# Maxima of the experts' scores: broadcast to all partitions and subtracted in PSUM, instead of a product with a row of ones

## The chip, the cores and the metric

The kernel runs on one core of a Trainium2 chip. The metric is the device time in microseconds of one execution, as the median of several. A core has five engines that run their own queues of instructions: TensorE (PE in the profile; PEld is its weight load), VectorE (DVE), ScalarE (ACT), GpSimd (POOL) and SyncE (SP, which here issues all DMAs but one).

## The reference

Two stages follow each other. The first is attention in clusters for 4 x 8 heads of 768 positions and 64 channels. The second, which the change is about, takes the first one's output as `x` (4 x 768 x 512) and computes for each of four experts a causal attention with one head of 64 channels, weighted by a gate:

```python
for e in range(E):
    q = x @ wq[e]
    k = x @ wk[e]
    v = x @ wv[e]
    scores = scale * (q @ k.transpose(0, 2, 1))
    scores = np.where(causal, -1000000000.0, scores)
    scores = scores - scores.max(-1, keepdims=True)
    a = np.exp(scores)
    a /= a.sum(-1, keepdims=True) + 1e-09
    ye = a @ v @ wo[e]
    for kk in range(K):
        mask = topk[:, :, kk] == e
        out += mask[..., None] * w[:, :, kk:kk + 1] * ye
```

The weights `wq` and `wk` are scaled up some 53 times, so the scores are large and the maximum of each row has to be taken off before the exponential.

## The kernel before

The work is cut into 24 steps. Steps 0 to 15 are the first stage, each a pair of heads of one batch. Steps 16 to 23 are the experts: four batches times two pairs of experts, so a step holds two experts (`h` = 0, 1), one in partitions 0 to 63 and one in 64 to 127. 128 x 128 products in full width (projections, line 773; values, 813; output, 1305) use the whole array. The products of two experts of 64 channels use it in two halves of 64 rows, side by side.

In an expert step the scores are made twice. First with the query on the partitions (line 970, `moe_maxes`), so that DVE can reduce each row to its maximum: a custom instruction that adds the causal mask and takes the maximum on the diagonal block (line 978), a plain reduction elsewhere (981). The 12 columns of maxima (`M6`) are transposed by PE (1076), copied from PSUM with the sign turned (`mr`, 1082 or 1085), and one small DMA puts them as a row each into partitions 0 and 64 of a tile `qm`, whose other partitions are zero. Then the scores are made once more with the key on the partitions (line 1003, `moe_scores`), as the softmax's sum and the product with the values need them. Here four terms add up in PSUM: three for the product of numbers split in a high and a low part, (kh, qh), (kl, qh) and (kh, ql), and as the fourth a product of a tile `kone`, which holds ones in partitions 0 and 64 and zeros elsewhere, with `qm`. It adds minus the maximum of each query to each key. ACT then takes the exponential straight out of PSUM (1017), POOL cuts the diagonal block to the causal part (1158), PE multiplies with the values (1191), and DVE or POOL adds up the sums (375, 376).

A step has nine such score tiles (`hf` is the half of the queries, `kc` the block of 128 keys): five of 2 x 384 columns, two of 2 x 256 and two of 2 x 128. Each takes a pair of PSUM's eight banks (`bank2`, four pairs), out of the same eight that all other products use.

The order of all operations on all engines is written out by hand: `SEQ` lists some 3,700 numbers of operations, with a letter where an operation goes to another engine than its first choice (`a`, `d`, `p` for ACT, DVE, POOL), and `SLOT` says which bank or buffer each gets. `Plan.run` issues the operations in that order, and each engine works through its own in sequence. While the scores and sums of one expert step run, the projections of the next and the output of the one before stand between them.

Of the kernel before, what the change touches and what calls it, by code (L numbers as in the profile page):

```python
# [10 lines left out]
def _warn_once_fixed(msg, *args, **kwargs):  # L11
# [26 lines left out]
23 15 64 0 14 5 4 32 28 40 45 46d 47d 48p 41 43 27 6 37 38 42d 49 50 51 52 1 13 53 55 56 12 57 231 234 25 232 20 222  # L38
223 225 224 2 31 22 19 227 228 34 394 44p 70 39 58 59 60 61 399 400d 235d 30 62 63 233d 67 68 69 66 229 24 9 395 396
77 78 79 80 81p 82p 71 237 238 36 35 3 239 29 8 21 16 73 33 65 7 401 397 72 74 76p 75p 10 11 104 90 108 100 17 88 18  # L40
26 240 241 89 109 242 243 403 106 406 407 404 405 101 92 93 105 244 96 97 111 245 409 410 107 98 102 256 99 114 115
86 411 91 94 95 87 103 110 257 252 253 566 83 152 153 173 148 149 168 169 85 84 130 131 157 174 158 126 127 112 122
123 128 129 575 54 230p 246 248 249 418 247 113 163 124 138 125 139 254 164 258 260 132 133 422 421 166 167 255p
398p 161 162 259p 412 413 150 151 146 147 154 226p 251 402p 423 171 172 134 136 118 155 120 121 135 119 116 156 160
176 159 165 170 175 117 137 140 141 310 311 281 298 414 415 142 143 177 299 285 304 305 282 306 307 144 145 416 417
261 269 270 300 200 201 207 208 424 425 426 427p 263 428 429 197 419 301 420 202 203 264 286 236 267 268 180 198 191
430 432 433 431p 277 278 182 183 302 195 308 309 181 250 262 196 184 185 275 276 205 192 206 292 279 280 303 271 186
187 188 571 296 297 293 290 294 295 189 190 193d 199 204 209 576 577 578 579 283 284 265 266 572 273 288 194 210 211
573 272 289 291 312 274 287 313 460 435 436 314 315 462 463 480 482 483 567 568 434 474 481 443 457 458 441 442 569d
475 581 582 212 213 444 737 592 593 178 179 461 214 215 447 439 355 372 356 373 379 380 437 438 362 363 440 583 357  # L50
325 584 448 585 326 346 364 358 365 327 367 368 344 345 472 331 316 317 318 359 360 347 332 453 454 574p 570p 594
353 354 361 366 586 587 369 370 445 466 468 469 377 378 455 456 467 473 329 322 446 330 341 476 477 342 323 319 324
588 589 908 470 471 216 374 375 336 334 320 321 337 328 464 595 596 738 599 600 335 601 371d 602p 591 746 449 478
479 339 450 597 598p 742 743d 451 452 459 382 383 340 349 739 333d 338d 465 484 485 486 376d 381d 343d 348 590 603
604 217 649 650 635 408 647 648 605 487 740 741p 749 750 747 628 624 625 629 620 636 621 218 909 945 384 748 752 351
352 653 654 626 627 385d 386 744 763 745p 764 765 387 534 616 617 549 550 525 526 527 651 753d 614 615 531 633 634
528 532 608 609 350 544 545 631 632 536 641 642 652 529 530 612 610 611 503 504 613 516 517 541 542 754 755 497 518
519 535 491 537 546 547 492 493 494 495 496 756 539 488 637 638 489 511 513 490 514 540 533 220 643 954 618 498 499
580 219 538 644 619 512 757 500 758 645 646 501 502 506 606 607 507 388 759 760 639 622 551 552 761 950 951d 508 509
770 766 767 768 771 772 775 762 774 505 510d 515d 520d 946 554 521 773 769 947d 543d 640 623 655 630 656 657 555 952  # L60
1116 389 658 522d 955 956 957 958d 781 785 814 818 779 819 815 780 390 922 776 786 782 548 553 556 557 523 524 558
1125 948 972 971 923 392 391 953p 949p 973 960 961 820 804 799 800 805 707 708 705 812 824 821 825 698 808 674 675
# [3 lines left out]
718 1117 978 979 980 974 975 560 976d 982 1121 681d 981 827 828d 1122d 983 977 561 829 984 751 714d 719d 723 724d  # L66
725 726 685 683 692 693 686d 691d 1123d 1124p 1128 1129d 1118 1119 562 1126 1127 830 1022 1023 1028 1005 993 994
1006 694 727 728 1131 1132 695d 729 1296 1120p 1144 1142 564 563 730 1029 1024 989 990 855 856 999 1000 1030 1031
1025 839 840 841 848 833 834 835 849 1133 1134 853 1135 869 870 831 832 871 872 836 1016 843 844 888 889 1007 837
838 995 1017 996 845 846 854 858 1136 1137 1143 1001 1002 860 861 842 847 987 988 731 1008 850 851 1026 1138 1139  # L70
1140 1010 997 998 1011 1141 565 1287 959 859 863 864d 852 857 862 1145 1149 1150 1151 1152p 985 891 892 1003 867 868
1146 1147 1148p 1154 732 1153 1027 1014 1004 881 1015 1155 991 883 884 1018 1019 893 894 1020 1032 878 879 992 986
1009 1033 1021 873 1012 1013 1034 886 1044 874 875d 1292 882 876 877 880d 885d 1297 1288 1035 1299 1300 1293 1036
1037 887 1289 896 1290 1298 1302 890d 1458 895d 898 899d 1294 1295p 1303 865 1467 866 900 1314 733 1313 1291p 897
# [4 lines left out]
1319 1326 1060d 734 1195 1066 1189 1067 1071 1065 1070 1181 1470 1076 903 904 1130 736 1190 1072 1471 1196 1185 1186  # L79
1086 1203 1182 1162 1204 1163 1087 1081 1082 1468 1469 1178 1197 1179 1180 1083 1088d 1093d 1463 1096 1097 1187 1188  # L80
# [3 lines left out]
1362 1363 1333 1334 1475 1227 1228 1255 905 1466p 1462p 393 1486 1250 1251 1476 1356 1357 1340 1477 1234 1235 1248  # L84
1249 1229 1230 1257 1256 1258 1254 1259 1270 1271 1360 1372 1373 1337 1358 1239 1260 1240 1261 1265 1266 1264 1478
1479 1215 1216 1217 1352 1224 1225 1212 1480 1481 1361 1634 1359 1109 1638 1482 910 1483 1301 1345 1338 1346 1370
1371 1272 1273 1630 1213 1214 1221 1491 1492 1493 1222 1341 1353 1376 1487 1488 1267 1489 1490 1237 1223 1226d 1494
1495 1496 1635d 1631d 1268 1269d 1238 1242 1275 1276 1110 1342 1523 1351 1377 1378 1111 1497 907 1243 1274 1231d
1236d 1241 1379 1112 1113 1114 1636d 1632 1655 1639 1514 1640 1524 1525 1516 1517 1641 1386 1545 1546 1541 1542 1535
1536 1642 1644 1645 1277 1278d 1244 1800 1245d 1279 1643 1656 1280 1637p 1633 1657 1533 1534 1502 1503 1526 1393  # L90
# [3 lines left out]
1540 1658 1659 1281 1428 1429 1521 1662 1663 1664d 1665 1430d 1435d 1654 1809 1282 1660 1666 1667 1283 1403 1518  # L94
1498 1441 1442 1404 1436 1437 1504 1543 1544 1397d 1440d 1519 1445d 1413 1547 1661 1402d 1668 1446 1499 1505 1414
# [111 lines left out]
    vt="010101011010101011011100010110",  # L207
    mx="0110100110101010101001010110010101010101",
    ssb="010101010101010101010101",
    acc="010101010101010101010110011010011001",  # L210
    avu="010101010101010101011010",
    r="0101010101010101010110010",
    xt="0100010101010101010101100110100110100",
# [3 lines left out]
    g="01320123",  # L217
# [1171 lines left out]
```

## Time and profile before

| | before |
|---|---|
| median of 3 runs | 673.76 us (673.62 to 674.83) |
| the profiled execution | 673.12 us, its span 671.4 us |
| PE busy | 663.9 us (99%) |
| PEld busy | 513.6 us (76%) |
| DVE busy | 543.4 us (81%) |
| ACT busy | 340.1 us (51%) |
| POOL busy | 302.7 us (45%) |
| granted TensorE clock | 0.999 of 2.4 GHz |

A busy share is the time in which an engine had an instruction in work. Matmuls are pipelined: the next starts before the last ends, so what a product costs in a stream is the distance of two starts and not its own duration. The distance between the end of the span and the execution's own time is 1.7 us.

### The profile page before, as it was taken

The numbers are of one execution on the slowest core, as the hardware profiler recorded it, in microseconds if no ns is written. First come the engines' busy times: TensorE is split into PE (matmuls) and PEld (weight loads), VectorE is DVE, ScalarE is ACT, GpSimd is POOL, SyncE is SP. The second block draws the span as 40 slices with busy tenths as digits, with TensorE's granted clock in tenths as the row PEclk, the third lists the DMA queues.
The fourth block names the chain that finished last, engine by engine and source line by source line (L and its number), as shares of the span: only waits on it lengthen the run. The fifth ranks groups of instructions, "written<-read, shape, count | busy, mean of one in ns | idle before, by whom it ended". The sixth has DMA issues, their size and how long they took to land.

```text
span 671.4 us, 13404 instructions
## 1 busy us (share of the span) xinstructions
PE 663.9 (99%) x4817; PEld 513.6 (76%) x4817; DVE 543.4 (81%) x1210; ACT 340.1 (51%) x791; POOL 302.7 (45%) x275
## 2 busy tenths in 40 slices
PE   9999999999999999999999999999999999999997
PEld 6778677677677677687687688969969969968975
DVE  7998998988799979999999988669576857786543
ACT  4556466467576466465575543264324334426423
POOL 4885555473664563536577132236132365304200
PEclk9999999999999999999999999999999999999999
DMA  6796868687678578577767533220322010221232
GB/s 200 182 219 140 207 167 181 169 206 195 161 205 202 143 199 230 149 176 193 164 173 189 142 97 99 69 72 2 96 95 73 28 50 25 74 73 50 95 121 95
DMA packets 70735, 90.79 MB, mean 135 GB/s; under 512 B 21088, under 2 KB 60428, under 8 KB 70668
## 3 DMA queue, kind: packets, MB, share of 16 engines
q1 hardware_dynamic: 70524, 89.90, 51.4%
q8 instruction: 38, 0.62, 0.4%
q14 instruction: 29, 0.24, 0.1%
q10 hardware_dynamic: 144, 0.03, 0.0%
HBM read 36.54 MB, written 12.91 MB: 74 GB/s over the span
## 4 chain that ended last, share of the span: by engine, by line
PE 87%; DVE 10%; issue 1%; ACT 1%; POOL 1%; DVEq 0%; ACTq 0%
PE banks L1191 19%; PE banks L773 10%; PE banks L1055 10%; PE banks L1134 8%; PE banks L1135 8%; PE banks L1003 6%; PE banks L813 5%; PE banks L1305 5%; DVE acc L376 3%; PE banks L516 3%; PE banks L1215 2%; PE banks L970 2%; DVE mx L1061 2%; PE banks L1138 1%; PE banks L1143 1%; PE banks L547 1%
## 5 line engine op out<-in xcount | busy, mean ns | idle before, releaser
L1061 DVE TENSOR_REDUCE mx<-banks 128x1 f32<-128x384 f32 x384 | 190.7, 547 | 13.2 <-PE banks L1055 11.8
L1134 PE MATMUL banks<-tq,tk 128*128 128x384 f32 x324 | 113.9, 352 | 0.0
L1055 PE MATMUL banks<-tk,tq 80*128 80x384 f32 x384 | 111.3, 358 | 0.1
L1135 PE MATMUL banks<-tq,tk 97*128 97x384 f32 x324 | 109.7, 339 | 0.0
L1153 ACT ACTIVATE p<-banks 128x384 f32<-128x384 f32 x144 | 65.4, 497 | 25.9 <-PE banks L1135 21.1
L1055 PEld LDWEIGHTS banks<-tk,tq 80*128 80x128 f32 x384 | 67.5, 189 | 11.6 <-DVE mx L1061 5.2
L1134 PEld LDWEIGHTS banks<-tq,tk 128*128 128x128 f32 x324 | 61.2, 189 | 6.4 <-issue 1.5
L1135 PEld LDWEIGHTS banks<-tq,tk 97*128 97x128 f32 x324 | 61.6, 190 | 0.0
L370 ACT ACTIVATE avu<-banks 128x384 f32<-128x384 f32 x34 | 16.5, 487 | 72.1 <-PE banks L1191 67.3
L978 DVE CUSTOM_DVE_ANT_0 banks<-banks,tri 128x384 f32<-128x384 f32 (+4 forms) x96 | 45.6, 530 | 5.7 <-PE banks L970 4.8
L1191 PE MATMUL banks<-p,vt 128*64 128x384 f32 x288 | 50.0, 490 | 0.0
L1266 POOL TENSOR_TENSOR xt<-avu,rb 128x384 f32<-128x384 f32 x28 | 28.2, 1023 | 48.2 <-DMA rb<-rd 27.4
L1153 ACT ACTIVATE xl<-banks 128x384 f32<-128x384 f32 x88 | 42.1, 500 | 8.6 <-PE banks L1135 7.7
L375 POOL TENSOR_TENSOR acc<-acc,p 128x768 f32<-128x768 f32 x16 | 29.9, 1868 | 34.0 <-DVE acc L376 32.6
L1003 PE MATMUL banks<-tk 64*128 64x384 f32 (+2 forms) x432 | 43.7, 311 | 0.1
L1153 ACT ACTIVATE xh<-banks 128x384 f32<-128x384 f32 x80 | 38.0, 501 | 4.4 <-PE banks L1135 3.9
L1191 PEld LDWEIGHTS banks<-p,vt 128*64 128x64 f32 x288 | 19.8, 137 | 24.6 <-issue 21.2
L375 POOL TENSOR_TENSOR lo<-xk,hi 128x384 fp32r<-128x384 f32 x28 | 27.9, 1009 | 22.0 <-DVE mx L1061 8.9
L1003 PEld LDWEIGHTS banks<-tk 64*128 64x128 f32 x432 | 34.7, 185 | 1.7 <-issue 0.4
L375 POOL TENSOR_TENSOR wvh<-wvh,p 128x768 f32<-128x768 f32 x12 | 21.9, 1824 | 20.6 <-DVE wvh L376 19.7
L1191 PE MATMUL banks<-xl,vt 128*64 128x384 f32 x176 | 30.8, 488 | 0.0
L370 ACT ACTIVATE tk<-banks 128x384 fp32r<-128x384 f32 x16 | 7.8, 491 | 42.8 <-PE banks L773 42.8
(313 smaller groups left out, 1684.0 us busy)
## 6 DMA issues: line engine op xcount, KB each, us to landing
tk<-hi SPq DMA_DIRECT2D x60, 192.0 KB
tq<-hi SPq DMA_DIRECT2D x56, 192.0 KB
rb<-rd SPq DMA_DIRECT2D x46, 192.0 KB
vt<-in_v_dram SPq DMA_DIRECT2D x16, 384.0 KB
x<-xt SPq DMA_DIRECT2D x16, 384.0 KB
kt<-in_k_dram SPq DMA_DIRECT2D x15, 384.0 KB
qt<-in_q_dram SPq DMA_DIRECT2D x15, 384.0 KB
tk<-lo SPq DMA_DIRECT2D x30, 192.0 KB
```

The lines of the kernel that those rows point to most:

```text
L375: ways = [("pool", t_pool(n), lambda: POOL.tensor_tensor(dst(), a(), b(), op=fn)), ("dve", t_dve(n), lambda: DVE.tensor_tensor(dst(), a(), ...
L773: PE.matmul(m()[:, :HW], w_()[:, dc, es], x_[dc]()[:, js], start=(i == 0), stop=(i == 3 * DC - 1))
L813: PE.matmul(m()[:, :NV], x_[dc]()[:, ts], w_()[:, dc, :], start=(i == 0), stop=(i == 3 * DC - 1))
L978: DVE.tensor_tensor_reduce(ps()[:, h, :w], ps()[:, h, :w], tri[:, 512 - w:], 1.0, -3.0e38, OP.add, OP.max, to)
L1003: PE.matmul(p()[:, h, o_:HW], kone[0][r] if a is None else a()[r, ks], b()[r, qs], start=(j == 0), stop=(j == 3))
L1055: PE.matmul(ps()[:, :w], Q[0:R, 0, h, c * 128:(c + 1) * 128], K[0:R, 0, h, i * w:(i + 1) * w], start=True, stop=True)
L1061: DVE.tensor_reduce(mx()[:, h, cc, i:i + 1], ps()[:, :w], axis=AX.X, op=OP.max)
L1134: PE.matmul(p()[:, o_:HW], K[:, 1, h, ks], Q[:, 1, h, qs], start=True, stop=False)
L1135: PE.matmul(p()[:, o_:HW], K[0:R, 0, h, ks], Q[0:R, 0, h, qs], start=False, stop=True)
L1153: ACT.activation(pt()[:, h, po:po + w], p()[:, o_:HW], AF.Exp, scale=SC)
L1191: PE.matmul(av()[h * 64:(h + 1) * 64, o_:HW], d["vv"](h, kc), pt()[:, h, po:po + HW - o_], start=(kc == 0), stop=(kc == nk - 1), tile_posi ...
L1305: PE.matmul(m()[:, :n1 - n0], a_()[:, ts], w_()[:, ep, n0:n1], start=(ep == 0 and i == 0), stop=(ep == EP - 1 and i == 2))
```

## The change

The fourth term goes: `kone`, the tiles `qm` and the memsets that clear them are dropped, and a score tile has three terms. The maxima keep their sign. `mr` is written to a DRAM tile `md`, and two DMAs read it back, one for each half of the queries, with the same row going to all 128 partitions (2 experts x 384 queries, 384 KB in SBUF each). A DVE instruction on each score tile subtracts this tile from the scores in PSUM, in place, before ACT takes the exponential. The broadcast tiles are `hi` and `lo` in even steps, and in odd ones two of the tiles that held the first stage's keys (`KEEP`), which leave the ring of buffers for the exponentials. No score product waits for the maxima any more; the subtraction does.

```diff
+    KEEP = ["tk02", "tk03"]
...
+    def max_tiles(n):
+
+        if n % 2:
+            return [late_tile(x) for x in KEEP]
+        return [(tmp(x, (128, 2, HW)), []) for x in ("hi", "lo")]
...
-        def part(first, last):
-            def go():
-                for j in range(first, last):
-                    for h in range(2):
-                        r = slice(h * D, (h + 1) * D)
-                        a, b = [(kh, qh), (kl, qh), (kh, ql), (None, qm)][j]
-                        PE.matmul(p()[:, h, o_:HW], kone[0][r] if a is None else a()[r, ks], b()[r, qs],
-                                  start=(j == 0), stop=(j == 3))
-            return go
+        def go():
+            for j, (a, b) in enumerate(((kh, qh), (kl, qh), (kh, ql))):
+                for h in range(2):
+                    r = slice(h * D, (h + 1) * D)
+                    PE.matmul(p()[:, h, o_:HW], a()[r, ks], b()[r, qs], start=(j == 0), stop=(j == 2))
...
+        s_ = op("pe", 3 * t_mm(w), go, due, d["st_ready"], [p, kh, kl, qh, ql], mode="r")
         d["st"].append(s_)
+
+        def go():
+            DVE.tensor_tensor(p()[:, :, o_:HW], p()[:, :, o_:HW], mb()[:, :, o_:HW], op=OP.subtract)
+        s_ = op("dve", t_dve(2 * w), go, due + 0.2, [s_, m_op], [p, mb])
...
+                if moe:
+                    md = dram.tile([2, 2, HW], FT, name=f"md{n}")
+
+                    def go(mr=mr, md=md):
+                        dma(md.rearrange("h f (c p) -> (h f c) p", p=128), mr())
+                    o = op("sp", [(0.42, 1.1, 0.18)], go, due + 0.5, [o], [mr])
+                    for i, (mb, free) in enumerate(max_tiles(n)):
+                        def go(i=i, mb=mb, md=md):
+                            dma(mb(), md[:, i][None].to_broadcast([128, 2, HW]))
+                        m_ops.append((op("sp", [(0.6, 2.65, 1.8)], go, due + 2.5 + i, [o] + free, [mb]), mb))
+                    continue
```

The table `SEQ` is another one from about step 10 on, and so are the banks in `SLOT`. The numbers of operations per kind stay, but for those named above; of the operations that may run on either of two engines in the expert steps, 29 go from DVE to POOL and 9 back, 35 from DVE to ACT and 30 back. The last line of the table:

```diff
-3706 3707 3714 3708 3709 3715 3716 3717 3722 3723 3724 3725
...
+3770 3784 3785 3786 3771 3772 3773 3774
```

Where the products stand now is best seen in the order of each engine. On PE, a stretch of score products of an odd step before, with the maxima's products (970) of the next step between them (`tk` holds a step's keys and queries, `lo` is `qm`, `cbd` is `kone`; x6 is three terms for two experts):

```order
L813 MATMUL banks<-wvl_4278,xh_0_5695 128x260
L970 MATMUL banks<-tk_96 128x128 x2
L970 MATMUL banks<-tk_96 128x256 x2
L1003 MATMUL banks<-tk_98 128x128 x6
L1003 MATMUL banks<-lo_5273,cbd 128x128 x2
L1003 MATMUL banks<-tk_98 128x384 x6
L1003 MATMUL banks<-lo_5273,cbd 128x384 x2
L970 MATMUL banks<-tk_96 128x384 x2
L1003 MATMUL banks<-tk_98 128x384 x6
```

And the same engine after, in score products of an odd step (994 is now the score product, 963 that for the maxima, 807 the values):

```order
L994 MATMUL banks<-tk_98 128x256 x6
L994 MATMUL banks<-tk_98 128x384 x12
L963 MATMUL banks<-tk_96 128x512 x2
L807 MATMUL banks<-wvh_4198,xh_0_5748 128x260
L807 MATMUL banks<-wvh_4198,xl_0_5794 128x260
L807 MATMUL banks<-wvl_4279,xh_0_5748 128x260
```

Before, all nine tiles of that step stand in one stretch of 64-row products; after, two or three score tiles stand between products of full width, twelve of line 807 in this case.

On SP, the rows around the DMA of the maxima in an even step (20) before:

```order
L358 DMA vt_6324<-x_117 128x768
L358 DMA hi_4786<-mr_6272 2x6x128
L358 DMA vt_6481<-x_114 128x768
L358 DMA sd<-ssb_6316 4x1x192 x2
L358 DMA r_6563<-sd 128x12
```

and after:

```order
L361 DMA vt_6273<-x_114 128x768
L361 DMA md_141<-mr_6275 12x128
L361 DMA lo_6278<-md_141 128x2x384
L361 DMA hi_6280<-md_141 128x2x384
L361 DMA out_dram<-xt_6312 128x512
```

One DMA of 6 KB became one of 6 KB to DRAM and two that write 384 KB each, the second half's queries being fetched first here or there.

On DVE after, a piece of the same step: the subtractions (line 1000) stand between the instructions that reduce the next step's rows (971; `ISA` is the custom instruction):

```order
L971 ISA M_101 128x1
L1000 TENSOR_TENSOR banks<-banks,lo_6278 128x2x384
L1000 TENSOR_TENSOR banks<-banks,hi_6280 128x2x128
L1000 TENSOR_TENSOR banks<-banks,hi_6280 128x2x256
L971 ISA banks,mx_6293<-banks,tri 128x320
```

Rows of line 1000 have no counterpart before.

## Rows read from the trace of the kernel before

**Rows 1.** Busy us by stretch: PE, PEld, DVE, ACT, POOL; clock, DMA share, GB/s

```profile
300.00:350.00 50.00, 49.93 (x341) 36.97 (x339) 47.88 (x98) 30.72 (x76) 31.35 (x25) 1.00 0.72 173
...
500.00:525.00 25.00, 25.00 (x245) 22.56 (x243) 17.01 (x58) 12.07 (x25) 6.86 (x8) 1.00 0.19 64
...
sum 225.00, PE 224.50 PEld 188.34 DVE 155.28 ACT 93.95 POOL 71.95; mean PE 24.94 PEld 20.93 DVE 17.25 ACT 10.44 POOL 7.99
```

**Rows 2.** Waits of PEld for exponentials, 425 to 655 us: total us, times, longest

```profile
PEld banks L813 <- ACT tk L1017: 0.4, 1, 0.4
...
PEld banks L1215 <- ACT tq L1017: 0.2, 1, 0.2
```

**Rows 3.** Line 1003, the fourth terms: count, min/median/max ns, first and last start, forms

```profile
L1003 PE MATMUL banks<-hi,cbd x72: 269/333/338, 450.8 to 620.5; 64*128 64x384 f32 x40, 64*128 64x128 f32 x16, 64*128 64x256 f32 x16
L1003 PE MATMUL banks<-lo,cbd x72: 270/333/338, 469.8 to 624.1; 64*128 64x384 f32 x40, 64*128 64x256 f32 x16, 64*128 64x128 f32 x16
```

**Rows 4.** Timeline of PE in a stretch of score products: start us, us

```profile
505.06 0.34 PE L1003 MATMUL banks<-hi,cbd 64*128 64x384 f32 x2
505.23 0.74 PE L1003 MATMUL banks<-tk 64*128 64x384 f32 x6
...
505.94 0.74 PE L1003 MATMUL banks<-tk 64*128 64x384 f32 x6
...
507.15 0.33 PE L1003 MATMUL banks<-hi,cbd 64*128 64x256 f32 x2
507.27 0.50 PE L1003 MATMUL banks<-tk 64*128 64x128 f32 x6
...
508.79 0.28 PE L1003 MATMUL banks<-hi,cbd 64*128 64x128 f32 x2
508.90 0.56 PE L1003 MATMUL banks<-tk 64*128 64x384 f32 x4
```

**Rows 5.** Timeline of PE where the shape of the products changes

```profile
423.88 0.28 PE L813 MATMUL banks<-wvh,xl 128*128 128x260 f32 x1
424.00 0.28 PE L813 MATMUL banks<-wvl,xh 128*128 128x260 f32 x1
424.21 0.76 PE L970 MATMUL banks<-tk 64*128 64x128 f32 x6
...
425.69 0.61 PE L970 MATMUL banks<-tk 64*128 64x384 f32 x4
426.23 0.45 PE L773 MATMUL banks<-xh,wqh 128*128 128x384 f32 x1
426.51 0.33 PE L773 MATMUL banks<-xl,wqh 128*128 128x384 f32 x1
```

**Rows 6.** Groups by line and form: busy us, mean ns, idle before

```profile
L1017 ACT ACTIVATE tq<-banks 128x768 f32<-128x768 f32 x23 | 18.4, 811 | 3.5 <-PE banks L1003 3.2
...
L981 DVE TENSOR_REDUCE mx<-banks 128x2 f32<-128x768 f32 x8 | 7.6, 956 | 3.4 <-PE banks L970 3.4
```

**Rows 7.** Timeline: a product for the maxima, and its reduction that waited for it

```profile
509.65 0.34 PE L970 MATMUL banks<-tk 64*128 64x384 f32 x2
...
510.10 0.96 DVE L981 TENSOR_REDUCE mx<-banks 128x2 f32<-128x768 f32 x1 [2.23 <-PE banks L970]
```

**Rows 8.** Timeline: a row to DRAM, its two broadcasts, and their first reader

```profile
581.58 0.80 SPq L358 DMA_DIRECT2D rd<-r  x2
...
583.48 1.15 SPq L358 DMA_DIRECT2D rb<-rd  x2
...
587.52 0.96 DVE L376 TENSOR_TENSOR avu<-avu,rb 128x768 f32<-128x768 f32 x1 [1.28 <-DMA rb<-rd]
```

**Rows 9.** Timeline of the last steps: sums of step 22 out and back, first product of the last output

```profile
640.50 1.11 SPq L358 DMA_DIRECT2D sd<-ssb  x2
...
645.66 0.34 SPq L358 DMA_DIRECT2D r<-sd  x1
...
659.35 0.50 PE L1305 MATMUL banks<-s,kt 128*128 128x512 f32 x1
```

More of the change, by code (lines that the diff above doesn't have):

```diff
@@ L43 @@
[L43 to L47, printed above, removed]
@@ new lines @@
+2750 2751 2758 2752 2762d 2776 2771 2772 2769 2770 2790 2774 2781 2768 2767d 2773d 3076 2900 2959d 2960 2846 2777
+2775 2778d 2780 2782 2784 2791 3077 3078 2976 2977 2783d 2785 2799 2800 2792 2793 2788 2789 2794 2795 2796d 2815
+2808 2805 2803 2797 2813 2798 2806 2802 2801d 3082 3083d 3084 2809 2804 2816 2814 2811 2807d 2812 2817 2923 2924
+2925 2905 2906 2907 2901 2818 2819 2902 2903 2974 2975 3079 3080 3081p 2920 2941 2942 2786 2787 2820 2821 2822 2943
+2944 2921 2922 2908 2926 2936 2937 2938 2911 2912 2913 2931 2932 2933 2927 2928 2929 2930 2934 2935 2914 2939 2940
@@ L209 @@
+    vt="010101011010101100000011101001",
+    mx="0110100110101010101001010101011010101010",
     ssb="010101010101010101010101",
[L210 to L213, printed above, removed]
+    acc="010101010101101001011010011010010110",
+    avu="010101010101010110010101",
+    r="0101010101010101010101010",
+    xt="0100010101010101110001100011110001011",
     mr="01010101010101010101010",
-    vm="011010110101",
+    vm="011011001010",
@@ L731, in late_part, with late_tile @@
         return late_tiles[nm][:, j]
-    def max_rows(n):
-        if n % 2 not in rows_of:
-            rows_of[n % 2] = tmp(("hi", "lo")[n % 2], (128, S), FR)
-        return rows_of[n % 2]
+    def late_tile(tag):
+        t = plan.buf(lambda _: late_part(tag), tag, (128, S), FT)
+        t.view = lambda a: a.rearrange("p (h c) -> p h c", h=2)
+        return t, P[NA - 3 + (int(tag[2]) - 1) % 3]["st"]
+    def max_tiles(n):
+        if n % 2:
+            return [late_tile(x) for x in KEEP]
+        return [(tmp(x, (128, 2, HW)), []) for x in ("hi", "lo")]
     def moe_operands(n):
@@ L742, in moe_operands @@
         i = 1 + n % 2
-        kh, kl, qh, ql = [plan.buf(lambda _, j=j: TK[i][:, j // 2, j % 2], f"o{i}{j}", (128, S), FR) for j in range(4)]
-        qm = max_rows(n)
-        d["ops"] = kh, kl, qh, ql, qm
+        d["ops"] = kh, kl, qh, ql = [plan.buf(lambda _, j=j: TK[i][:, j // 2, j % 2], f"o{i}{j}", (128, S), FR) for j in range(4)]
         xh, xl, xo = X[b]
         free = P[NA - 3 + n % 2]["st"] if n < NA + 2 else []
-        zero = []
-        if n < NA + 2:
-            def go():
-                POOL.memset(qm().bitcast(FT), 0.0)
-            def go_one():
-                kone.append(consts.tile([128, 256], FR, name="cbd")[:, :128])
-                for r, x in ((slice(0, 128), 0.0), (slice(0, 1), 1.0), (slice(D, D + 1), 1.0)):
-                    POOL.memset(kone[0][r].bitcast(FT), x)
-            zero = [op("pool", 0.75, go, t0 - 46, use=[qm])]
-            if n == NA:
-                zero.append(op("pool", 0.4, go_one, t0 - 46, [P[NA - 1]["cent"]]))
         es = slice(ep * 128, (ep + 1) * 128)
@@ L923 @@
     LATE = [f"tq{i}{j}" for j in range(4) for i in (1, 2)] + [f"t{x}0{j}" for j in range(4) for x in "kq"]
+    LATE = [x for x in LATE if x not in KEEP]
     late_free = {}
@@ L953, in moe_maxes @@
         d = P[n]
-        kh, kl, qh, ql, qm = d["ops"]
+        kh, kl, qh, ql = d["ops"]
         out = []
@@ L988, in moe_maxes, with moe_scores @@
         return out
[L990 removed]
+    def moe_scores(n, hf, kc, o_, po, pt, due, m_op, mb):
         d = P[n]
[L993 removed]
+        kh, kl, qh, ql = d["ops"]
         p, w = bank2(), HW - o_
         ks, qs = slice(kc * 128, (kc + 1) * 128), slice(hf * HW + o_, (hf + 1) * HW)
[L997 to L1013 removed]
+        def go():
[3 more added lines that the diff above has]
+                    PE.matmul(p()[:, h, o_:HW], a()[r, ks], b()[r, qs], start=(j == 0), stop=(j == 2))
+        free = late_free.pop(pt, [])
+        s_ = op("pe", 3 * t_mm(w), go, due, d["st_ready"], [p, kh, kl, qh, ql], mode="r")
         d["st"].append(s_)
+        def go():
+            DVE.tensor_tensor(p()[:, :, o_:HW], p()[:, :, o_:HW], mb()[:, :, o_:HW], op=OP.subtract)
+        s_ = op("dve", t_dve(2 * w), go, due + 0.2, [s_, m_op], [p, mb])
         def go():
@@ L1078, in core, with go_a, go_d @@
                 d["m_pe"] = [o, o]
-                mr = tmp("mr", (2 * NC, 128), FR, bufs=2)
-                def go_a(m=m, mr=mr):
-                    ACT.activation(mr(), m()[:2 * NC, :128], AF.Copy, scale=-1.0)
-                def go_d(m=m, mr=mr):
-                    DVE.tensor_scalar(mr(), m()[:2 * NC, :128], -1.0, None, op0=OP.mult)
-                o = op("act", t_act(128), go_a, due + 0.4, [o], [m, mr], alt=("dve", t_dve(128), go_d))
+                mr, sign = tmp("mr", (2 * NC, 128), FT if moe else FR, bufs=2), 1.0 if moe else -1.0
+                def go_a(m=m, mr=mr, sign=sign):
+                    ACT.activation(mr(), m()[:2 * NC, :128], AF.Copy, scale=sign)
+                def go_d(m=m, mr=mr, sign=sign):
+                    DVE.tensor_scalar(mr(), m()[:2 * NC, :128], sign, None, op0=OP.mult)
+                o = op("act", t_act(128), go_a, due + 0.4, [o], [m, mr], alt=("dve", t_dve(128), go_d))
+                if moe:
[8 more added lines that the diff above has]
+                    continue
                 def go(mr=mr):
-                    dma(qm()[0:65:64] if moe else Q[MR:MR + 1, 0].rearrange("p h s -> p (h s)"), mr())
-                o = op("sp", [(0.84, 1.14, 0.15)], go, due + 0.5, [o] + (d["zero"] if moe else sets_free(n)), [mr, qm] if moe else [mr])
+                    dma(Q[MR:MR + 1, 0].rearrange("p h s -> p (h s)"), mr())
+                o = op("sp", [(0.84, 1.14, 0.15)], go, due + 0.5, [o] + sets_free(n), [mr])
                 m_ops = 2 * [2 * [[o]]]
@@ L1126, in core @@
                     pt = p_tile(n)
-                exps = moe_scores(n, hf, kc, o_, po, pt, due, m_ops[hf][0]) if moe else []
+                exps = moe_scores(n, hf, kc, o_, po, pt, due, *m_ops[hf]) if moe else []
                 for h in () if moe else range(2):
```

307 lines of the change are left out of this document (146 added, 161 removed), and 40 rows, old and new, of the table SEQ.

## The prediction

> **What bounds the kernel now.** I read busy time by stretch first. In the experts' stage, 425 to 650 us, PE has an instruction in work for 224.50 of 225 us, DVE for 155.28, ACT and POOL for less than half [rows 1]. Since the busy time of pipelined matmuls can hide pauses, I then read the timeline of starts: score products for two experts follow each other every 0.178 us for 384 columns, group after group [rows 4], and full-width products of 260 columns every 0.12 [rows 5]. That leaves no room: PE really is the bound. The list of waits confirms it: for exponentials of score tiles PE's weight loads wait in seven groups of 0.4 down to 0.2 us, 1.8 us in all [rows 2]. So a product that goes is worth its interval, and whatever else makes PE pause costs its full length.
>
> **What goes.** The fourth term is 144 instructions, 72 pairs that run side by side: 40 pairs of 384 columns, 16 of 256 and 16 of 128 [rows 3]. A pair's worth is the distance between two starts: eight products of a tile take 505.94 - 505.23 = 0.71 us, or 0.178 a pair; the pair of 256 takes 507.27 - 507.15 = 0.12, that of 128 takes 0.11 [rows 4]. The sum is 40 x 0.178 + 16 x 0.12 + 16 x 0.11 = 10.8 us, all of it on the path. The memsets of the ones and the rows go too; they stand once on POOL, long before their use, and are worth nothing.
>
> **What moves on PE.** The new order no longer lets the score products of a step stand in one stretch. I counted in both orders how often a product has another shape than the one before it (full width, 64 rows, 64 columns, 32 columns): 115 times before, 160 after; stretches of 64-row products grow from 15 to 39. What a change costs is in rows 5. A full-width product starts 0.12 us after the one before, but the first 64-row product 0.21 after it: 0.09 more. The two pairs at 425.69 take 0.54 us instead of 0.355: 0.185 more. The first full-width product of 384 columns behind them holds its place 0.28 us, against 0.178 at most: 0.10 more. A visit to the 64-row shape thus costs 0.38 us for two changes, 0.19 each. 45 more changes make 8.6 us. The bounds are 0.09 (4.1 us), the entry alone, and 0.29 (13.1 us), if the whole 0.185 belonged to the exit; I take 0.19, the mean over a whole visit, as most added changes come in such visits.
>
> The Trainium skill says in "TensorEngine Tiling (Array Packing)", section Key Properties, that changing the tiling mode drains TensorE. The trace agrees, with the 0.38 us per visit above; the page gives no figure. Without that rule one would forecast the full 10.8 us.
>
> **What comes on DVE.** 72 subtractions, 40 of them on 768 columns. The nearest row is a reduction of 768 columns in PSUM, 0.956 us [rows 6]. By columns alone 72 subtractions are 40 x 0.956 + 16 x 0.64 + 16 x 0.32 = 54 us, with each at the full 0.956 they are 69; I take 56, near the first. Twenty additions net leave DVE for POOL at about as much each, 19 us. DVE then has 155 + 56 - 19 = 192 of 225 us, 85%. The first stage runs at 47.88 of 50 us on DVE with PE at 49.93 [rows 1], so this load alone does not slow PE.
>
> But a score tile now keeps its pair of banks longer: before until its exponential ends (0.811 us [rows 6]), now for the subtraction too, 0.956 + 0.811 and three hand-overs of 0.11 (a product ends at 509.99, its reduction starts at 510.10 [rows 7]): 2.1 us. I added up, with the intervals above, the products that stand in the new order between each score product and the next one that writes its banks. For nine of 72 they are too few, by 1.5 us in all; in the old order by nothing. In return the closed stretches go in which PE waits for exponentials; of the 1.8 us there I take half as gone. That is +0.6 us net; it could be -1.8, if no new wait came, and what it could be at most is the first rival.
>
> **What comes on SP.** The maxima go to DRAM and come back twice to all partitions. A row to DRAM until its broadcast is issued took 583.48 - 581.58 = 1.9 us, two broadcasts of 192 KB until their reader ran 4.0 [rows 8]. The new ones write 384 KB each, so 4.0 to 8.1 us, if time went by bytes; I take 5, since the row's 4.0 holds much that does not depend on size (its two issues are 1.15 of it). From `mr` to the first subtraction that makes some 7 us, where one small DMA stood. No PE product waits for it; the subtraction does, and behind it on DVE stand the reductions of the next step's rows. By the same sum of products the new order puts most scores 9.5 us or more behind the transposed maxima in steps 16 to 19 and 21, and the first ones of steps 20, 22 and 23 at 5.4 to 8.2 us. There one to three tiles stand filled in PSUM for 1 to 2 us; I cost it at nothing, as full-width products follow them on PE.
>
> **The sum.** -10.8 + 8.6 + 0.6 = -1.6 us against the profiled execution's 673.12 us (span 671.4 and 1.7 around it), so 671.5. That execution lies 0.64 us below the median of the runs shown, 673.76, so on the median's scale I forecast 672.2 us. A measurement of this kernel can tell about 0.2% from no change, 1.35 us: the forecast is faster by little more than that.
>
> **Rivals.**
>
> *PSUM runs short and PE waits for DVE: slower.* The place is the 39 stretches of score products. A wide tile takes PE 3 x 0.178 = 0.53 us, and DVE and ACT 0.956 and 0.811 to clear, and all products share eight banks. If each of the eight steps showed one full subtraction, 8 x 0.956 = 7.6 us, the sum would be -10.8 + 8.6 + 7.6 = +5.4, or 679.2 us. It decides from waits of 3.6 us on (0.09 per stretch), where the loss passes 1.35. For it: PE and two other engines now stand in a ring, and nine distances are short already. Against: DVE has 15% left, and only nine of 72 are short. On this the Trainium skill, again in "TensorEngine Tiling (Array Packing)", section PSUM Bottleneck, says that tiling speeds up TensorE but not the clearing of PSUM; this trace shows it only as the few waits named first.
>
> *Changes of shape cost the entry alone: faster.* At 0.09 each the sum is -10.8 + 4.1 + 0.6 = -6.1, or 667.7 us. For it: part of what I counted around 425.69 may be a weight load that any first product shows. Against: the distances at entry, inside and behind all stand in one stretch, and add up.
>
> *The broadcasts land late: slower.* If time went by bytes, 8.1 us, the first subtractions of steps 20, 22 and 23 would wait 1.9 + 8.1 - 6.8 = 3.2 us longer than their products, with the next step's reductions behind them. Half of that reaching PE, in three steps, makes +4.8 on the forecast: 677.0 us. Against: DMA is at 19% in that stage [rows 1].
>
> *The end comes out: no change.* Sums of step 22 go out at 640.50 and the first product that needs them starts at 659.35, 18.9 us later. Of these, 5.2 us pass before the second DMA at 645.66 [rows 9], where the like took 1.9 in rows 8, so 3.3 are SP's queue. In the new order I count 14.5 us of products in between. Without the queue the chain is 15.6, so 1.1 us would show: 673.3 us. Against: DVE's order around it also changes, and the chain has more slack than I can see.
>
> **How the numbers follow.** The forecast has 0.54, with a range of its own of 670 to 674.5; by the bound it splits into 0.29 faster, 0.21 within, 0.04 slower. The cheap changes have 0.15 (0.15 faster), PSUM 0.15 (0.01 within, 0.14 slower), the late broadcasts 0.09 (slower), the end 0.07 (0.04 within, 0.03 slower). Faster is then 0.44, same 0.26, slower 0.30. The range has to take in the cheap changes below and most of the two slower cases above: 667 to 678.5 us, with some 0.05 left out below and 0.1 above.
>
> **What would show it.** Line 994 in place of 1003 should have 432 products at the same intervals, so that tiles of 384 columns follow at 0.53 us. Around each visit of the 64-row shape I expect 0.38 us more than the intervals. Subtractions (line 1000) should take 0.95 us for 768 columns, and PE's list of waits should show them with less than some 3 us in all, DVE 80 to 90% busy from 425 to 650. The stage should be shorter by about 2 us, the first one unchanged. The forecast is wrong if PE waits for subtractions or their exponentials by more than 3 us, if a visit costs 0.2 us or 0.6, or if PE has gaps before the last output's products.

## The result: slower by 1.4%, and the profile after

| | before | after |
|---|---|---|
| median, side by side | 674.30 us (4 runs) | 684.45 us (682.83 to 684.76, 4 runs) |
| ratio, 95% interval | 1 | 1.0143 [1.0119, 1.0167] |
| profiled execution, span | 671.4 us | 683.0 us (684.73 us in all) |
| mean granted clock | 0.999 | 0.993 |
| DVE, POOL busy | 543.4, 302.7 us | 580.0, 330.4 us |

The forecast, 672.2 us and most likely faster, was wrong: 10.15 us were lost, and the time lies outside the range. Of 67 executions of the kernel before, 15 have a mean granted clock of 0.992 and take some 5 us longer than the others (0.996 or more), so each median below stands beside that of the kernel before, measured together with it.

Busy us by stretch of the kernel after, columns as in [rows 1], the last line being the sum of 425 to 650 us:

```profile
550.00:575.00 25.00, 21.34 (x154) 13.44 (x150) 22.47 (x48) 9.82 (x18) 15.43 (x14) 0.93 0.26 78
...
650.00:683.00 33.00, 29.28 (x210) 21.45 (x208) 14.67 (x34) 9.43 (x19) 1.89 (x5) 0.90 0.23 78
...
sum 225.00, PE 220.31 PEld 176.21 DVE 183.52 ACT 96.24 POOL 99.47; mean PE 24.48 PEld 19.58 DVE 20.39 ACT 10.69 POOL 11.05
```

Against [rows 1] DVE has 28 us more, spread over the stage, and PE 4 us less, nearly all of that in one stretch, 550 to 575. There and in the last 33 us the granted clock is below 1.00; in all others it is 1.00. So two places stand out, and I looked at each.

The first place. PE's timeline, with the idle time ahead of an instruction and what ended it in brackets:

```profile
557.83 1.46 PE L1190 MATMUL banks<-tq,vm 128*64 128x384 f32 x12
562.40 0.32 PE L963 MATMUL banks<-tk 64*128 64x128 f32 x1 [3.10 <-DVE M L971]
...
562.92 2.79 PE L994 MATMUL banks<-tk 64*128 64x384 f32 x18
565.63 2.58 PE L1190 MATMUL banks<-tq,vm 128*64 128x384 f32 x12
```

PE stands still for 3.1 us for a reduction of line 971. Then the 12 products of line 1190 take 2.58 us instead of 1.46, as the clock has fallen. On DVE, this is what stands ahead of that reduction:

```profile
553.31 0.17 DVE L828 TENSOR_REDUCE sm<-lg 128x6 f32<-128x24 f32 x1
553.51 0.71 DVE L829 TENSOR_TENSOR oh<-lg,sm 128x24 f32<-128x24 f32 x1
554.26 1.77 DVE L830 TENSOR_TENSOR oh<-oh,ramp 128x24 f32<-128x24 f32 x1
556.06 0.18 DVE L831 TENSOR_REDUCE sm<-oh 128x6 f32<-128x24 f32 x1
556.27 0.99 DVE L832 TENSOR_TENSOR oh<-oh,sm 128x24 f32<-128x24 f32 x1
557.30 1.74 DVE L834 SCALAR_TENSOR_TENSOR oh<-oh,lg 128x24 f32<-128x24 f32 x1
...
561.74 0.55 DVE L971 CUSTOM_DVE_ANT_0 banks<-banks,tri 128x384 f32<-128x384 f32 x1
```

They are the first six of the gate's twelve small instructions (lines 828 to 836). All twelve, up to line 971, take 8.4 us, where two other groups of the gate in this trace take 2.4. POOL at the same time:

```profile
552.37 1.81 POOL L378 TENSOR_TENSOR acc<-acc,p 128x768 f32<-128x768 f32 x1
554.14 1.85 POOL L378 TENSOR_TENSOR xl<-vt,xh 128x768 fp32r<-128x768 f32 x1
555.94 1.28 POOL L378 TENSOR_TENSOR acc<-tq 128x512 f32<-128x512 f32 x1
557.18 1.82 POOL L378 TENSOR_TENSOR acc<-acc,p 128x768 f32<-128x768 f32 x1
```

Line 830 ends at 556.03, POOL's addition at 555.99; 832 at 557.26, POOL's at 557.22; 834 at 559.04, POOL's at 559.00: each waits for an addition of POOL to end and is done 0.04 us later. The reductions 828 and 831, with one input, keep their 0.18 us beside the same additions. The Trainium skill states this in "SBUF — State Buffer", section Who interferes with whom: a DVE instruction with two inputs in SBUF contends with a POOL instruction that reads SBUF, as the second input comes over a read interface that the two engines share. The rows agree.

The prediction did not weigh this, though the trace of the kernel before has it already, in an earlier group of the gate:

```profile
462.30 1.29 POOL L375 TENSOR_TENSOR acc<-tk,tq 128x512 f32<-128x512 f32 x1
...
462.48 1.16 DVE L840 SCALAR_TENSOR_TENSOR oh<-oh,lg 128x24 f32<-128x24 f32 x1
...
464.04 1.85 POOL L375 TENSOR_TENSOR acc<-acc,tq 128x768 f32<-128x768 f32 x1
...
464.11 1.82 DVE L836 TENSOR_TENSOR oh<-oh,ramp 128x24 f32<-128x24 f32 x1
```

Both end 0.04 to 0.05 us behind an addition, and that group takes 4.9 us; PE did not pause for it. So the collision is not new, and the 29 operations that the change hands to POOL are not its main cause: of the seven additions beside the group in the kernel after, POOL made six before too, as the letters in `SEQ` say. Only one (`3237d` before, `3269` after) was handed over, and the wait for it is 1.0 of the 6 us lost. What is new is the place: the group now stands beside all seven, and ahead of reductions that PE needs at once.

The second place is the end. PE's timeline from the last values on (lines 887 and 889 are sums of one column for the last step):

```profile
660.79 1.72 PE L887 MATMUL banks<-ones,acc 128*128 128x1 f32 x14
...
664.45 0.99 PE L887 MATMUL banks<-ones,acc 128*128 128x1 f32 x4
665.37 3.25 PE L1190 MATMUL banks<-tq,vm 128*64 128x384 f32 x16
668.41 2.37 PE L903 MATMUL banks<-identf,r 128*64 128x128 f32 x24
670.71 0.50 PE L1304 MATMUL banks<-s,kt 128*128 128x512 f32 x1
```

And the clock there, a column of the stretches (last but two):

```profile
660.00:665.00 5.00, 5.00 (x39) 4.44 (x35) 3.32 (x7) 0.84 (x1) 0.00 (x0) 0.84 0.19 55
665.00:670.00 5.00, 5.00 (x35) 3.79 (x36) 2.13 (x7) 0.49 (x1) 0.00 (x0) 0.50 0.02 3
```

In the row of 32 one-column products (the expected texts say 28) the clock falls to 1.2 GHz, at 663.4, and stays there for 6.8 us. Before, the like products stood with 12 full-width output products between them.

The subtractions, with the columns of [rows 6]:

```profile
L1000 DVE TENSOR_TENSOR banks<-banks,tk 128x768 f32<-128x768 f32 x20 | 18.5, 962 | 0.2 <-PE banks L994 0.2
```

A subtraction of 768 columns takes 0.96 us. The maxima's way through DRAM cost nothing: in the list of what DVE waits for, line 1000 has PE (3.5 us) and ACT (0.7) but no DMA.

### The profile page after: what moved, and what is told of

Read it like the earlier page. It is cut to its first block, busy times and chain, and to the rows that moved or that the text cites. A ratio compares the mean times of both kernels' runs of the same rounds, so it can differ in the third digit from the quotient of the medians.

```text
span 683.0 us, 13218 instructions
## 1 busy us (share of the span) xinstructions
PE 669.9 (98%) x4673; PEld 507.6 (74%) x4673; DVE 580.0 (85%) x1251; ACT 348.3 (51%) x801; POOL 330.4 (48%) x291
## 5 line engine op out<-in xcount | busy, mean ns | idle before, releaser
L378 POOL TENSOR_TENSOR acc<-acc,p 128x768 f32<-128x768 f32 (+2 forms) x23 | 38.2, 1662 | 55.9 <-PE banks L994 31.2
L1004 ACT ACTIVATE tq<-banks 128x768 f32<-128x768 f32 (+2 forms) x47 | 31.0, 675 | 22.4 <-DVE banks L1000 21.8
L994 PE MATMUL banks<-tk 64*128 64x384 f32 (+2 forms) x432 | 41.7, 322 | 0.5 <-DVE M L971 0.3
L378 POOL TENSOR_TENSOR acc<-acc,tq 128x768 f32<-128x768 f32 (+2 forms) x18 | 25.9, 1442 | 12.7 <-ACT tq L1004 10.6
```

What stands on the lines that cost most here:

```text
L378: ways = [("pool", t_pool(n), lambda: POOL.tensor_tensor(dst(), a(), b(), op=fn)), ("dve", t_dve(n), lambda: DVE.tensor_tensor(dst(), a(), ...
L994: PE.matmul(p()[:, h, o_:HW], a()[r, ks], b()[r, qs], start=(j == 0), stop=(j == 2))
L1004: ACT.activation(pt()[:, :, po:po + w], p()[:, :, o_:HW], AF.Exp, scale=SC)
```

## The experiments

**What makes the pause?** e1 moves the gate's group in the order of operations (3347 is that group, 3457 a later reduction). e5 moves it further, together with the exponential behind it (3348), to behind the last reduction and to where POOL waits; the second cut shows e5 against the changed kernel:

```diff
-... 3453 3347 3060 ...
-... 3456 3457 ...
+... 3453 3060 ...
+... 3456 3347 3457 ...
```

> The changed kernel with one operation moved: the first group of small DVE instructions of the gate of the third batch (lines 828 to 836, 553.31 to 561.8 us in the trace after) goes behind two reductions and four subtractions of the next steps, to where POOL has nothing in work and DVE waited 2.15 us. Theory A (these instructions wait for POOL's additions, the reductions behind them are late, PE stands still for 3.1 us and then has half the clock for some 4 us): the wait of PE at 559.3 goes, the granted clock stays at 1.00 between 540 and 575 us, these instructions take 2.4 us, and the time falls by 4 to 7 us, to 677.5 to 680.5 us. Theory B (DVE has too much to do with the subtractions, and whatever stands there makes it late): the wait only moves to another product, and the time stays within 1.5 us of 684.5.

Measured: 680.73 us (before: 675.26; ratio 1.0071 [1.0048, 1.0094]), just above A's range. One collision was still there; on DVE, POOL and PE:

```profile
564.84 1.65 DVE L832 TENSOR_TENSOR oh<-oh,sm 128x24 f32<-128x24 f32 x1
...
564.65 3.60 POOL L378 TENSOR_TENSOR xl<-vt,xh 128x768 fp32r<-128x768 f32 x2 [2.21 <-ACT xh L373]
...
567.09 0.79 PE L1304 MATMUL banks<-s,kt 128*128 128x512 f32 x1 [2.53 <-DVE mx L971]
```

The collision explains at most 1.65 - 0.18 = 1.5 of PE's 2.53 us here. The remaining 1.0 comes from the group's own 2.2 us, as it still stands ahead of a reduction that PE waits for.

```diff
-... 3453 3347 3060 ...
-... 3072 3348 3061 ...
-... 3398 3402d ...
+... 3453 3060 ...
+... 3072 3061 ...
+... 3398 3347 3348 3402d ...
```

> The changed kernel with the same group of the gate's instructions moved further than in e1: behind all reductions of that step, ahead of an addition that POOL waits for, so that POOL has nothing in work there. In e1 one of them still stood beside an addition of POOL (line 832, 1.65 us at 564.84) and ahead of two reductions, and PE waited 2.53 us. Theory A (the collision is the whole of the pause): PE has no wait over 1 us between 540 and 575 us, the granted clock stays 1.00 there, and the time is 5.5 to 7.5 us below the changed kernel's 684.5, 677 to 679. Theory B (DVE is simply late there): a wait of 2 us or more and the low clock stay, 680 us or more.

Measured: 677.73 us (before: 675.91; 1.0000 [0.9968, 1.0033]), 6.7 below the changed kernel. PE has no wait over 0.3 us from 400 us on, and the stretch is full at full clock:

```profile
550.00:575.00 25.00, 25.00 (x201) 18.18 (x200) 18.78 (x55) 11.99 (x23) 18.95 (x19) 1.00 0.35 113
```

That is theory A's outcome. The edit takes the group out of POOL's way and from ahead of the reductions at once, so it does not part the two. In the changed kernel the group lost 6 us to POOL and PE stood still for 3.1, so there the collisions are enough to explain the pause. e3 shows from the other side that the subtractions are not the cause of the pause:

```diff
-            DVE.tensor_tensor(p()[:, :, o_:HW], p()[:, :, o_:HW], mb()[:, :, o_:HW], op=OP.subtract)
+            pass
```

> The changed kernel without its 72 subtractions: ACT takes the exponential straight out of PSUM (with a smaller scale, so that numbers stay finite); the maxima are still reduced and broadcast, but nothing reads them. Order, banks and engines of all else stay. Theory A (the subtractions themselves cost little; the loss is in the new order's changes of shape, in the gate's instructions that wait for POOL and in the end): 675 to 681 us. Theory B (the load of 59 us on DVE and the longer hold on PSUM are the loss): 674 us or less, as then only about 9 us of changes of shape stand against 10.8 us of products saved.

Measured: 679.41 us (before: 675.26; 1.0055 [1.0025, 1.0085]), as A. In its waits of PE from 425 to 655 us (total, times, longest) the pause stands unchanged, with no subtraction anywhere:

```profile
PE banks L963 <- DVE M L971: 3.3, 2, 3.1
```

The time is 5.0 us below the changed kernel's all the same. Not all of that is the subtractions' own price: in e3's trace the low clock at the end lasts 3.4 us in place of 6.8.

**What are the subtractions and the order worth?** e9 is e5 with e3's edit.

> The kernel of e5 (gate's instructions behind the reductions) without its 72 subtractions: ACT takes the exponential straight out of PSUM, with a smaller scale, and nothing reads the broadcast maxima. Beside e5 it gives the price of the subtractions in the new order, beside e4 (old order, no fourth term, 668.7 to 671.7 where the clock held) the price of the new order itself. Theory A (the new order's 45 more changes of shape cost 0.2 us each, 9 us, and it saves the 6 us or so for which PE waits for exponentials in the old order's closed stretches): 672 to 675 us, and the subtractions cost 2 to 5 us of e5's 677.7. Theory B (the new order is as good as the old without its pauses, and the subtractions are what is left): 670 us or less, subtractions 7 us or more.

Measured: 675.54 us (before: 675.04; 0.9987 [0.9967, 1.0007]), a little above A's range. Beside e5 the subtractions cost 2.2 us. And the new order, with nothing to subtract and no pause, is no faster than the kernel before, though it has 10.7 us fewer products: its changes of shape and the low clock at its end, both below, take that back. e4 is the same for the old order:

```diff
-                for j in range(first, last):
+                for j in range(first, min(last, 3)):
```

> The kernel before without its fourth term: the 144 products with the row of ones are left out, the maxima are still reduced and sent, but nothing reads them (the exponential has a smaller scale, so that numbers stay finite). Order, banks and engines of all else stay. Theory A (PE is the bound and a product is worth its interval): 674.3 - 10.8 = 663.5 us, within 1.5. Theory B (without these products PE waits for exponentials in the closed stretches of scores, as a tile comes from PE every 0.53 us and ACT needs 0.81): 667 us or more.

Measured: 670.64 us (before: 675.26; 0.9935 [0.9905, 0.9965]): theory B. PE in one closed stretch of scores, its first row and the one behind it, in the kernel before and then in e4:

```profile
468.70 0.62 PE L970 MATMUL banks<-tk 64*128 64x256 f32 x4
...
476.06 0.86 PE L1215 MATMUL banks<-acc,ones 128*32 128x192 f32 x16
```

```profile
470.08 0.62 PE L970 MATMUL banks<-tk 64*128 64x256 f32 x4
...
477.38 0.86 PE L1215 MATMUL banks<-acc,ones 128*32 128x192 f32 x16
```

7.36 us before, 7.30 without its nine pairs of the fourth term (18 products less). The stretch lasts as long as before although PE has less to do. So PE waits there: by its weight loads 0.8 us for ACT's exponentials and 0.8 for DVE (a copy of keys and a reduction), against 0.2 each before. A product that goes is not worth its interval. This stretch is the extreme: over the whole stage PE's starts in e4's trace gain 4.2 of the 10.7 us. e8 puts a subtraction ahead of each exponential in that order, with the tile of the maxima's rows as it stands:

```diff
+            DVE.tensor_tensor(p()[:, :, o_:HW], p()[:, :, o_:HW], mb[:, :, o_:HW], op=OP.subtract)
             ACT.activation(pt()[:, :, po:po + w], p()[:, :, o_:HW], AF.Exp, scale=SC * 1e-6)
```

> The kernel before without its fourth term, as e4, but with a subtraction on DVE ahead of each exponential, in the old order with its closed stretches of scores. What is subtracted is the tile with the rows of maxima as it stands (zeros but for two partitions), with no broadcast, and the exponential has a smaller scale, so the numbers mean nothing; the wait for the maxima's DMA stays. Theory A (PSUM's clearing sets the pace of a closed stretch: 0.95 us on DVE and 0.81 on ACT for a tile that PE makes in 0.53, and so the new order had to break the stretches up): well above e4's 670, 678 to 690 us. Theory B (PE hides the subtractions in either order, and the new order only adds changes of shape): 676 us or less.

Measured: 725.40 us (before: 675.91; 1.0698 [1.0636, 1.0761]), A and far more. Waits of PE from 425 us on:

```profile
PE banks L1003 <- ACT tq L1019: 8.3, 14, 1.2
PE banks L1003 <- ACT tk L1019: 7.0, 5, 2.9
PE banks L970 <- ACT p L1019: 4.4, 3, 2.1
```

All waits of PE for these exponentials make some 30 us, and the granted clock fell to 0.962 on average, which is worth 725 x 0.038, some 28 us by estimate. So the old order can't take the subtractions as it stands: it loses 50 us. This is the prediction's PSUM rival, in the order that the change left. It agrees with what the prediction cited from the Trainium skill, "TensorEngine Tiling (Array Packing)", section PSUM Bottleneck: tiling speeds up TensorE but not the clearing of PSUM. Whether another order with closed stretches could hide the subtractions is not shown.

**What does a change of shape cost?** e12 adds a product of 64 rows ahead of the projections in the kernel before, e13 one of 128 rows:

```diff
                     i = 0
+                    PE.matmul(m()[:, :128], wh()[0:64, 0, es], xh[0]()[0:64, js][:, :128], start=True, stop=True)
                     for dc in range(DC):
```

> The kernel before with a product of 64 rows and 128 columns ahead of each of the 32 groups of 12 full-width projection products (line 773) in the experts' stage; the group's first product clears its result, so the output stays. 28 of the 32 stand behind a full-width product, so 56 changes of shape come in, with nothing that waits. With 0.19 us per change, as the forecast had it, this is 56 x 0.19 = 10.6 us above e13 (the same product in full width); at the entry's price alone, 0.09, 5.0; at 0.29, 16.2.

> As e12, but the added product has all 128 rows, so that no shape changes: the price of 32 products of 128 columns alone, 0.06 to 0.12 us each, 2 to 4 us above the kernel before (676 to 679).

Measured: e12 687.15 us (before: 675.21; 1.0202 [1.0165, 1.0238]), e13 678.24 (1.0053 [1.0017, 1.0089]). The difference is 8.9 us for 56 changes, 0.16 each. One visit in e12:

```profile
429.15 0.34 PE L1056 MATMUL banks<-tk,tq 80*128 80x384 f32 x1
429.43 0.32 PE L771 MATMUL banks<-xh,wkh 64*128 64x128 f32 x1
429.68 0.44 PE L774 MATMUL banks<-xh,wkh 128*128 128x384 f32 x1
429.96 0.34 PE L774 MATMUL banks<-xl,wkh 128*128 128x384 f32 x1
430.13 0.34 PE L774 MATMUL banks<-xh,wkl 128*128 128x384 f32 x1
```

A full-width product holds its place 0.175 us (429.96 to 430.13). The one ahead of the visit holds it 0.28 and the one behind it 0.28, 0.10 more each; the small product holds it 0.25, where e13 puts its worth at 0.095 ((678.24 - 675.21) / 32), 0.155 more. That is 0.36 a visit, 0.18 a change, near the forecast's 0.19.

**What is the end worth?** e2 cuts the row of one-column products in three with values between (3723 to 3761 are the sums, 3752 and 3720 values):

```diff
-... 3752 ... 3723 3722 ... 3759 3761 3724 3760 3720 ...
+... 3723 3722 3724 3752 ... 3759 3760 3720 3761 ...
```

> The changed kernel with another order of the last sums: the 28 one-column products of lines 887 and 889, which stand in one row at 660.8 us, are cut in three pieces with products with the values (line 1190) between them; nothing else moves. Theory A (in that row PE does so little that its clock falls to 1.2 GHz for the 5 us behind it): the granted clock stays near 1.00 until the last output's products, and the time falls by 2 to 4 us, to 680.5 to 682.5 us, less 0.8 us for four more changes of shape. Theory B (the end is a chain of sums, reciprocals and copies, and the clock only fills its pauses): the first product of the last output starts as long after the sums as before, and the time is within 0.8 us of 684.5.

Measured: 683.70 us (before: 675.26; 1.0124 [1.0083, 1.0165]), at B's edge. The clock was low for 3.4 us instead of 6.8, worth 1.7; four more changes of shape take back some 0.8 of that, by 0.19 each. e6 takes 12 output products from 648 us in between instead:

```diff
-... 3529 3530 ... 3541 3542 ...
-... 3723 3722 ... 3759 3761 ... 3724 ...
+... 3723 3541 3722 3542 ... 3759 3529 3761 3530 ... 3724 ...
```

> The changed kernel with 12 output products (line 1304), which stood between the last scores at 648 us, moved between the one-column products at the end, three at a time, as the kernel before has them; the gate is left where it is. Theory A (PE's clock falls because PE did little ahead of it): the clock stays 1.00 up to the last output, the 7 us at 1.2 GHz (663.7 to 670.7) go, and the time falls by 2.5 to 4 us, to 680.5 to 682. Theory B (the place at 648 needs them as cover for subtractions and additions, or the end waits for DVE): PE waits 2 us or more at 648, or the first product of the last output comes no earlier, and the time stays within 1 us of 684.5.

Measured: 693.83 us (before: 675.91; 1.0241 [1.0193, 1.0290]), and with e5's edit, in e7, 689.41 (1.0163 [1.0116, 1.0211]):

> Both edits, e5 and e6, together in the changed kernel. If the two places are the whole of what the forecast missed, the time is 684.5 - 6.5 - 3.3, some 674.5 us (673 to 676.5), within a third of a per cent of the kernel before, and the granted clock is 0.998 or more. If the loss lies in the subtractions all over the stage, it stays at 678 us or more.

Both are slower by e6's theory B and by a fault of my own making. The waits of PE in e6:

```profile
PE banks L903 <- DVE r L897: 5.4, 1, 5.4
...
PE banks L851 <- ACT tq L1004: 2.7, 1, 2.7
```

Without the outputs at 648 PE waits 2.7 us there; and two output DMAs that I moved stand on SP ahead of the row that the last reciprocals need, 5.4 us. In the row itself the clock stayed at 1.00. e10 brings the last additions forward and cuts the row once:

```diff
-... 3666 ... 3752 ... 3736d 3740d 3723 3722 ... 3759 3761 3724 3760 ...
+... 3736d 3740d 3666 ... 3723 3722 3724 3752 ... 3759 3761 3760 ...
```

> The kernel of e5 with a shorter end: two additions of the second half's sums stand ahead of the reciprocal (line 1242) that waits 1.86 us for its DMA on DVE, and the 12 one-column products of the first half ahead of eight products with the values, which cuts the row of 28 in two. Theory A (the end is slow as PE does little there and its clock falls): the last output's products start 1 to 2.5 us earlier against the sums (line 1214), and the time is 675 to 677 us, or equal to the kernel before. Theory B (the end hangs on the DMA of the last sums' reciprocals): no change against e5's 677.7.

Measured: 678.36 us (before: 675.04; 1.0055 [1.0036, 1.0074]), e5's time: the row begins 2 us earlier (652.0 against 654.1), but the clock falls there too, at 656.2 against 657.1, and is low for 6.8 us in both. e11 adds work instead:

```diff
+                wx = W["wo"][0]
+                PE.matmul(ps2()[:, :DM], wx()[:, 0, :128], wx()[:, 0, :DM], start=True, stop=True)
```

> The kernel of e5 with more work at its end: behind every one or two one-column products of the last sums stands one product of 128 x 512 whose result nobody reads, 12 in all, into a bank that lies free there. Theory A (the clock falls behind that row because PE did little in it): the granted clock stays 1.00 up to the last output, so that the 12 products, 12 x 0.23 = 2.8 us, are paid for by the 3 to 3.5 us that seven us at half the clock cost, and the time is 676 to 678.5, e5's 677.7 within 1 us. Theory B (the clock falls there anyway, or the end hangs on a chain that PE doesn't set): clock 0.995 as in e5, and the time is 2 to 3 us above e5's, or the same with the low clock still there.

Measured: 678.72 us (before: 675.21; 1.0061 [1.0038, 1.0083]). The two stretches in e5, and in e11:

```profile
655.00:660.00 5.00, 5.00 (x32) 4.09 (x33) 3.29 (x9) 0.84 (x1) 0.00 (x0) 0.71 0.00 0
660.00:665.00 5.00, 5.00 (x40) 4.30 (x37) 1.97 (x4) 1.29 (x3) 0.00 (x0) 0.61 0.02 3
```

```profile
655.00:660.00 5.00, 5.00 (x37) 4.61 (x36) 2.04 (x4) 0.84 (x1) 0.00 (x0) 1.00 0.02 6
660.00:665.00 5.00, 5.00 (x51) 3.90 (x51) 3.68 (x11) 1.08 (x3) 0.00 (x0) 1.00 0.02 3
```

With the 12 products the clock held. What that is worth is best read inside the two traces, from the row's first product to the first of the last output, in e5 and in e11:

```profile
654.10 1.72 PE L887 MATMUL banks<-ones,acc 128*128 128x1 f32 x14
...
664.02 0.50 PE L1304 MATMUL banks<-s,kt 128*128 128x512 f32 x1
```

```profile
654.69 0.38 PE L887 MATMUL banks<-ones,acc 128*128 128x1 f32 x2
...
664.23 0.50 PE L1306 MATMUL banks<-s,kt 128*128 128x512 f32 x1
```

That is 9.92 us in e5 and 9.54 in e11. With 12 x 0.23 = 2.8 us of products that nobody needs the end is 0.4 us shorter, so the low clock there costs some 3.2 us. By the medians, e11 1.0 above e5, it would be 1.8, but they are uncertain by a microsecond or two. Whether the clock falls does not hang on that row alone: in e4's trace, whose sums stand between output products as in the kernel before, it was 0.70 of full speed from 640 to 655 us. Why it fell there stays open.

No version that still takes the maxima off beat the kernel before: e5 equals it within what these runs can tell.

## Why the prediction was wrong

| term | forecast | measured | from |
|---|---|---|---|
| products of the fourth term | -10.8 | -10.7 | products by their intervals in both traces |
| 45 changes of shape | +8.6 | +9.0 (7.2 at e12's price) | 0.19 to 0.20 each in the trace after; 0.16 in e12 less e13 |
| subtractions, net waits | +0.6 | +2.2 | e5 less e9 |
| pause and low clock at 560 | 0 | +6.7 | after less e5 |
| low clock at the end | 0 | +3.2 (1.8 to 3.2) | e5 and e11, traces; 1.8 by their medians |
| sum | -1.6 | +10.4 | measured +10.15 |

- **PE is the bound; the fourth term is worth 10.8.** Right in the new order. In the old one only some 4.6 of it would have come (e4), as PE waits in its closed stretches for ACT and DVE; [rows 2], with 1.8 us of waits, does not show that, since the fourth term was what filled them.
- **Changes of shape, 0.19 each.** Right: 0.16 to 0.20 were measured.
- **"This load alone does not slow PE."** This is the step that failed. DVE's load was forecast at 85% and is 82% (183.5 of 225 us), and the subtractions cost 2.2 us. The load was right, the step from it was not. I judged DVE by its busy share over the stage, with each instruction at the time that it takes alone, and put what PE waits for DVE's reductions at nothing. In one place of the new order the gate's small two-input instructions stand beside seven additions of POOL and wait 6 us for them, and the reductions that PE needs stand behind. That cost 6.7 us (e5). The place was wrong too: not the 39 stretches but one. Of the operations handed to POOL, which I took as pure relief, one is among the seven.
- **The clock** stood in no term. Behind the pause of 3.1 us PE's products ran at 1.2 GHz for 3.4 us (564.4 to 567.8), which is 1.7 of the 6.7; shorter waits around it are the rest. And the end lost some 3.2 us with no pause in PE at all.
- **Rivals.** PSUM with PE waiting for DVE (679.2) came nearest in size. PE's wait in the pause was for banks that DVE had to clear, but of the maxima's products, not of scores, and not for want of time on DVE. The broadcasts came in time. The end came out, by the clock and not by the chain that I had added up. Changes of shape at the entry's price alone: e12 speaks against it, with 8.9 us where 0.09 each would make 5.0.
- **Signs.** 432 products, subtractions of 0.95 us, 0.4 us a visit and DVE at 80 to 90% came as said. The wait for exponentials passed its 3 us: in the list of [rows 2], in the same stretch, 12 groups with 6.5 us stand after in place of 7 with 1.8, the largest and one of the smallest being

```profile
PEld banks L963 <- ACT tq L1004: 1.6, 4, 0.6
...
PEld banks L1190 <- ACT tq L1004: 0.2, 1, 0.2
```

In e9 they are 2.1 us, so most of these waits are the subtractions', whose price is 2.2 us of the 10. For the reductions of the next step, which had the long wait, I had named no sign.

That the terms sum to 10.4 and not 10.15 says little: the medians that they come from were measured at different times and are uncertain by a microsecond or more.

## What to carry to other kernels

Where an order of work is made anew, look at which instructions of two engines stand side by side, not only at how full each engine is. Here DVE's small instructions paid for POOL's large additions, and what stood behind them on DVE made TensorE pause, which cost the pause and the clock behind it. The trace before had such a wait, and an instruction with two durations in one trace is the sign to look for. And before a product is dropped, ask what its stretch is waiting for: an interval read where another engine sets the pace is not what the removal gives.

## What was not expected of the hardware

- A DVE instruction of 24 columns, 0.18 us alone, took up to 1.77 us beside an addition of POOL, ending 0.04 us behind it; one-input reductions beside it kept 0.18 us. The kernel before shows the same, with 1.82 us.
- TensorE's granted clock fell to half in a row of 32 one-column products that follow each other at 0.11 us, in which PE counts as 100% busy; with 12 more products in that row it kept full speed in e11's trace.
